# Band attention and a GELU MLP on one core: sums of w_out's quarters by pieces, k of units 12 to 23 split in GpSimd's transfers, and a new order from unit 4 on

## The chip, the cores and the metric

The kernel runs on one NeuronCore of a Trainium2 chip. The metric is device time in microseconds (us) of one launch. Of the kernel before, the median of three runs is 560.4 us (560.36, 560.40 and 560.89).

Engines work side by side, each on its own queue, strictly in the order in which its instructions were issued: TensorE (PE; its weight loads are a column of their own, PEld), VectorE (DVE), ScalarE (ACT), GpSimd (POOL), and SyncE (SP), which issues most DMAs here.

## The reference

Attention over batch 4, 8 heads, 768 positions, head size 64; its output is cut into 3072 rows of 512 and goes through a two-layer MLP.

```python
k_sum = k.reshape(B, H, nb, block, D).max(axis=3)      # block = 32, nb = 24
v_sum = v.reshape(B, H, nb, block, D).mean(axis=3)
scores_l = where(|i - j| < 16, scale * q @ k.T, -1e9)  # the band
scores_s = scale * q @ k_sum.T + log(block)            # the summaries
a = softmax(concat([scores_l, scores_s]));  attn = a @ concat([v, v_sum])
x = attn.transpose(0, 2, 1, 3).reshape(3072, 512)
h = x @ w_in                                           # 512 -> 2048
g = 0.5 * h * (1 + erf(h / sqrt(2)))
out = g @ w_out                                        # 2048 -> 512
```

## The kernel before, in words

**Attention** is cut into 24 units of 256 queries by 4 heads. From unit 6 on (units 0 to 5 are f32) every f32 operand is split into two f16 parts, "hi" (the rounded value) and "lo" (what is left), and every product is three f16 products: hi by hi, hi by lo, lo by hi. A unit's steps are: load q, k, v; make their hi and lo parts; `scores` (TensorE, L861) into pss; `add_mask` (VectorE, L881); `maximum` (GpSimd); `shift` (VectorE, L895); `exponent` (ScalarE, L898); `s_p_hi` (ScalarE, L906) and `p_lo` (VectorE, L910); `sums` (TensorE, L959) and `values` (TensorE, L943); then `norm_take`, `norm_cross`, `norm_rec`, `norm_spread`, `norm_mult` (L966 to L993) divide by the sums, and `x_hi`, `x_lo` write the MLP's input xos. q of units 12 to 23 is split without VectorE: `q_cast` (GpSimd DMA that casts to f16, L829), `q_neg` (ScalarE, the negative, L833), `q_acc` (GpSimd DMA that adds the f32 values onto it, L836). k of all units comes by a DMA from SP (`load_k`, L689), its hi part on ScalarE (`s_k_hi`, L758), its lo part on VectorE (`k_lo`, L818). The maxima of k blocks (`prep_k`, L610, and `prep_k_end`) are copied beside k by `k_sums` (L623), once for the three units that share it.

**The MLP** works on 3072 tokens: six batches of 512 (0 to 5), of which the first two are worked on in four chunks of 256. Weights come as raw f32 and are cut into bits: `wi_bits` and `wo_bits` (L477, L482, L486), `wi_hi`, `wi_lo` (L512, L515), `wo_hi`, `wo_lo` (L572, L575). For w_out there are eight pieces, each 128x1024 f32. Chunks 0 to 3's first layer is `phase1` (L1020 to L1022, three products a row) into psh, then `gelu`, `g_hi`, `g_lo`; `phase2` (L1139 to L1141) into pso is the second layer of chunks 0 to 5 (batch 2 makes chunks 4 and 5), read by `store`. The first layer of batches 2 to 5 is done by Strassen's seven products: `xsum`, `xs_hi`, `xs_lo` (L1052 to L1063) make sums of x; `sp` (L1091) multiplies into psx, psy and psz; `snap` (L1102, ScalarE) empties a psy; `comb` or `h_comb` (L1109, L1194, VectorE) adds up; `h_gelu`, `h_sum`, `h_hi`, `h_lo` (L1199 to L1218) make the left operands of the second layer. Its second layer for batches 3, 4 and 5 is Strassen too: `so` (L1375) multiplies into pso_y, pss_x, psv_z and others; `o_snap` (L1397, ScalarE) empties a "y" accumulator into g_os; `o_sum` (L1404, VectorE) adds another accumulator to it; `o_out` (L1411) and `o_put` end it. In "so b n q j", b is the batch, n the product, q the quarter of the inner dimension, j the half of the columns; in "sp b q n" and "snap b q n", n is the product.

**Sums of w_out's quarters** are operands of that second layer. Before, they are made from w_out's hi and lo parts in SBUF: `t_sum q i` (32 VectorE additions of 128x512, L1295 and L1300), `t_hi`, `t_lo` (16 each, 128x512, L1328 and L1331), `ts` (16 DMAs into t_dram); `tl`, `tr` and `t1_load` load them back.

**What sets the order.** All steps stand in one hand-written list, `ORDER` (L79 to L272), some 2000 steps such as "so 3 7 3 1". They are issued in this order, and each engine runs its share in it. A step that has to wait holds everything behind it on the same engine. Buffers come from `SLOTS` (L273), digits that say which of a pool's buffers each new tile takes.

Of the kernel before, what the change touches and what calls it, by code (L numbers as in the profile page):

```python
# [103 lines left out]
prep_k 2 1, wo_bits 2 0, g_lo 1 3, wo_bits 2 1, norm_rec 4, phase2 0 0, wo_bits 2 2, g_lo 0 2, norm_spread 4,
load_mask, gelu 1 2, load_q 7, fetch_w_out 3 5, gelu 1 0, g_hi 1 0, wo_bits 3 0, gelu 0 7, prep_k_end 1 0, wo_bits 3
1, g_lo 1 1, wo_bits 3 2, phase1 0 6, phase1 1 7, k_sums 1 0, k_lo 6, load_vs 5, g_hi 1 2, fetch_w_out 4 4, shift 5,
s_q_hi 7, phase2 0 1, gelu 0 6, norm_mult 4, wo_hi 3, wo_hi 2, exponent 5, wo_lo 3, phase1 1 6, wo_bits 4 0,
fetch_w_out 5 5, wo_lo 2, wo_bits 4 1, scores 6, f_sums 5, evac 6, wo_bits 5 0, wo_bits 4 2, x_hi 4, wo_bits 5 1,
f_values 5, wo_hi 4, norm_take 5, norm_cross 5, wo_bits 5 2, wo_lo 4, f_mask 7, wo_hi 5, load_k 7, wo_lo 5, norm_rec
5, norm_spread 5, phase2 0 3, fetch_v 1 2, phase2 0 2, phase2 0 4, g_lo 1 0, x_lo 4, gelu 1 7, maximum 6, phase2 0 5,  # L110
load_v 7, norm_mult 5, q_lo 7, x_hi 5, g_hi 0 7, x_lo 5, s_k_hi 7, g_hi 0 6, g_lo 0 7, fetch_w_out 6 4, g_lo 1 2,
fetch_w_out 7 5, gelu 1 6, g_hi 1 7, fetch_k 1 2, shift 6, prep_v 1 2, wo_bits 6 0, phase1 2 6, g_lo 1 7, phase1 2 4,
gelu 2 6, exponent 6, gelu 2 4, phase1 2 0, g_hi 1 6, prep_k 1 2, wo_bits 7 0, load_v 6, k_lo 7, g_lo 0 6, prep_k_end
1 1, gelu 2 0, g_lo 1 6, load_k 9, s_p_hi 6, wo_bits 7 1, phase1 2 1, gelu 2 1, wo_bits 6 1, wo_bits 7 2, p_lo 6,
fetch_v 1 1, wo_bits 6 2, load_q 9, k_sums 1 1, phase1 2 7, fetch_v 1 0, wo_hi 7, wo_hi 6, s_q_hi 9, wo_lo 7, wo_lo 6,
scores 7, s_k_hi 9, sums 6, fetch_v 1 3, prep_v 1 1, q_lo 9, prep_v 1 0, fetch_k 2 0, fetch_v 2 1, prep_v 1 3, phase1
2 3, k_lo 9, fetch_k 2 3, load_vs 6, g_hi 2 4, phase2 0 6, store 0 0, phase2 0 7, g_hi 2 1, g_lo 2 1, g_lo 2 4,
norm_take 6, evac 7, load_q 8, prep_k 2 0, prep_v 2 1, phase2 1 0, g_hi 2 6, phase2 1 2, phase2 1 4, gelu 2 3, gelu 2
7, prep_k 2 3, norm_cross 6, load_vs 7, v_hi 6, maximum 7, load_k 8, wt_add 1 0, g_hi 2 7, v_hi 7, s_k_hi 8, wt_add 1
1, v_lo 6, fetch_v 2 2, shift 7, s_q_hi 8, v_lo 7, exponent 7, norm_rec 6, scores 9, values 6, load_v 9, prep_k_end 2  # L120
0, phase2 1 6, k_lo 8, q_lo 8, norm_spread 6, load_k 11, g_hi 2 3, prep_v 2 2, add_mask 9, s_p_hi 7, p_lo 7, load_q
11, maximum 9, norm_mult 6, wt_add 1 2, x_hi 6, phase1 2 5, g_lo 2 6, phase1 2 2, put 0 0, wt_hi 1, store 1 0, s_q_hi
11, scores 8, x_lo 6, gelu 2 5, add_mask 8, load_v 8, sums 7, norm_take 7, load_vs 9, norm_cross 7, put 1 0, wt_lo 1,
g_lo 2 7, fetch_k 2 2, shift 9, s_k_hi 11, norm_rec 7, q_lo 11, maximum 8, gelu 2 2, values 7, g_hi 2 2, v_hi 9,
phase2 1 1, norm_spread 7, phase2 1 3, store 0 1, g_hi 2 5, norm_mult 7, k_lo 11, x_hi 7, g_hi 2 0, g_lo 2 2, x_lo 7,
phase2 1 5, shift 8, exponent 8, v_lo 9, phase1 3 2, prep_k 2 2, g_lo 2 5, s_p_hi 8, phase2 1 7, load_q 10, p_lo 8,
s_q_hi 10, wt_add 0 0, g_lo 2 0, load_vs 8, v_hi 8, exponent 9, load_k 10, fetch_v 2 0, v_lo 8, load_v 11, phase1 3 4,
s_k_hi 10, sums 8, g_lo 2 3, scores 11, add_mask 11, load_v 10, wt_add 0 1, values 8, put 0 1, q_lo 10, wt_add 0 2,
phase1 3 5, gelu 3 2, load_vs 10, k_lo 10, norm_take 8, s_p_hi 9, p_lo 9, phase1 3 6, maximum 11, wt_hi 0, norm_cross
8, sums 9, scores 10, norm_rec 8, norm_spread 8, q_cast 12, load_k 12, gelu 3 6, store 1 1, norm_mult 8, gelu 3 5,  # L130
prep_v 2 0, load_vs 11, x_hi 8, add_mask 10, v_hi 10, values 9, norm_take 9, wt_lo 0, ws 0, norm_cross 9, g_hi 3 6,
put 1 1, shift 11, g_hi 3 2, gelu 3 4, x_lo 8, fetch_v 2 3, exponent 11, phase1 3 1, norm_rec 9, norm_spread 9, s_p_hi
11, norm_mult 9, maximum 10, q_neg 12, v_hi 11, k_sums 2 0, phase1 3 7, v_lo 10, phase2 2 1, g_lo 3 2, phase2 2 3,
shift 10, phase1 3 0, wt_add 2 0, v_lo 11, load_v 12, exponent 10, g_hi 3 5, p_lo 11, g_lo 3 5, sums 11, values 11,
phase2 2 5, s_k_hi 12, x_hi 9, prep_v 2 3, prep_k_end 2 1, gelu 3 0, k_lo 12, wt_add 2 1, wt_add 3 0, q_cast 13,
wt_add 2 2, k_sums 2 1, x_lo 9, norm_take 11, s_p_hi 10, p_lo 10, wt_add 3 1, q_acc 12, wt_hi 2, g_hi 3 0, scores 12,
gelu 3 1, phase2 2 7, g_lo 3 6, g_lo 3 0, add_mask 12, q_neg 13, norm_cross 11, load_vs 12, v_hi 12, g_hi 3 4,
norm_rec 11, load_k 13, wt_add 3 2, q_acc 13, norm_spread 11, maximum 12, sums 10, norm_mult 11, s_k_hi 13, norm_take
10, store 2 1, phase1 3 3, norm_cross 10, gelu 3 3, k_lo 13, phase2 2 0, v_lo 12, shift 12, sp 2 0 1, exponent 12,
norm_rec 10, g_hi 3 3, values 10, x_hi 11, wt_lo 2, load_v 13, s_p_hi 12, sp 2 0 2, load_k 15, snap 2 0 1, scores 13,  # L140
norm_spread 10, load_v 15, wt_add 6 0, wt_hi 3, x_lo 11, gelu 3 7, q_cast 15, norm_mult 10, put 2 1, fetch_k 3 3, p_lo
12, add_mask 13, phase2 2 2, phase2 2 4, xsum 2 1, xsum 2 3, xs_hi 2 3, g_hi 3 1, s_k_hi 15, xsum 2 2, wt_lo 3, xs_hi
2 2, g_lo 3 4, q_cast 14, sums 12, g_hi 3 7, sp 2 1 1, snap 2 1 1, phase2 2 6, xs_hi 2 1, comb 2 0 0, sp 2 1 2, prep_k
3 3, load_vs 13, v_hi 13, norm_take 12, store 2 0, k_lo 15, norm_cross 12, xs_lo 2 2, xs_lo 2 3, values 12, maximum
13, shift 13, t_sum 0 3, xsum 2 4, g_lo 3 3, wt_add 5 0, exponent 13, ws 1, s_p_hi 13, g_lo 3 1, wt_add 5 1, v_lo 13,
q_neg 15, comb 2 1 0, wt_add 6 1, load_k 14, norm_rec 12, sp 2 0 6, fetch_k 3 1, put 2 0, wt_add 5 2, prep_k 3 1,
s_k_hi 14, xs_hi 2 4, wt_add 6 2, k_lo 14, q_acc 15, snap 2 0 2, q_neg 14, load_v 14, phase2 3 0, phase2 3 2, wt_hi 6,
wt_add 7 0, xs_lo 2 1, load_k 17, wt_lo 6, sp 2 1 6, wt_add 4 0, sp 2 0 7, wt_hi 5, sp 2 0 5, p_lo 13, wt_add 7 1,
snap 2 1 2, snap 2 0 3, s_gelu 2 0 0, fetch_k 3 0, norm_spread 12, wt_add 4 1, phase2 3 4, s_gelu 2 1 0, norm_mult 12,
wt_add 4 2, q_acc 14, wt_hi 4, sums 13, xs_lo 2 4, comb 2 0 3, scores 15, sp 2 0 4, g_lo 3 7, s_k_hi 17, wt_lo 5,  # L150
wt_lo 4, s_gelu 2 0 2, sg_hi 2 1 0, phase2 3 6, norm_take 13, store 3 0, load_vs 15, sg_lo 2 1 0, k_lo 17, sp 2 1 5,
phase2 3 1, wt_add 7 2, norm_cross 13, load_vs 14, wt_hi 7, prep_k 3 0, sg_hi 2 0 2, norm_rec 13, add_mask 15, sp 2 0
3, wt_lo 7, scores 14, values 13, sg_lo 2 0 2, comb 2 0 1, s_gelu 2 0 3, fetch_v 3 0, v_hi 15, add_mask 14, sp 2 1 7,
# [1376 lines left out]
```

## Time and profile before

| what | value |
| --- | --- |
| median of three runs | 560.4 us |
| profiled execution | 560.75 us |
| its span | 558.9 us |
| TensorE (PE) busy | 549.5 us, 98% |
| VectorE (DVE) busy | 484.0 us, 87% |
| ScalarE (ACT) busy | 389.7 us, 70% |
| GpSimd (POOL) busy | 110.8 us, 20% |
| DMA packets' share of 16 engines, SP's queue | 43.3% |
| DMA packets' share, GpSimd's queue | 5.0% |

The span is the time from the first to the last recorded work on the core; 1.85 us of the profiled execution's own time lie around it. An engine's busy time is the union of its instructions' times, so matmuls that overlap are not counted twice. The granted clock of TensorE is 1.00 in all slices, its upper level of 2.4 GHz. Most rows are read as "start, duration, engine, line, operation, output <- input, shape, count"; a bracket at the end holds the idle time in front and what ended it. Durations of neighbours on one engine overlap at their ends by about 0.1 us.

### The profile page before, as it was taken

The page shows a single profiled execution, that of the slowest core. Times are in us where ns is not written, and L with a number is a line of the kernel's source. Part 1 is how long each engine was busy: PE and PEld are TensorE (multiplying, and loading weights), DVE is VectorE, ACT ScalarE, POOL GpSimd, SP SyncE. Part 2 cuts the span into 40 slices and gives each one's busy share as a digit, 9 for nine tenths or more (in the row PEclk, how much of TensorE's full clock was granted, in tenths as well). Part 3 has the DMA queues.
Part 4 walks back from the last instruction along what each step waited for, and adds up shares of the span by engine and source line. Part 5 has one row for each costly group of instructions (what it writes and reads, how often), then busy time and mean ns, then how long its engine had stood idle before and what let it go on. Part 6 is the DMA issues. An engine that isn't in the chain of part 4 may idle for free.

```text
span 558.9 us, 14486 instructions
## 1 busy us (share of the span) xinstructions
PE 549.5 (98%) x6155; PEld 414.8 (74%) x6155; DVE 484.0 (87%) x680; ACT 389.7 (70%) x677; POOL 110.8 (20%) x66
## 2 busy tenths in 40 slices
...
GB/s 328 396 285 380 166 173 178 280 116 221 157 146 171 153 143 187 133 65 182 127 167 149 154 115 89 90 145 200 256 207 150 60 94 1 1 1 29 48 1 86
DMA packets 42640, 84.26 MB, mean 151 GB/s; under 512 B 4176, under 2 KB 16720, under 8 KB 42064
## 3 DMA queue, kind: packets, MB, share of 16 engines
q1 hardware_dynamic: 38832, 79.85, 43.3%
...
q14 instruction: 16, 0.13, 0.1%
...
## 4 chain that ended last, share of the span: by engine, by line
PE 81%; DVE 13%; DMA 3%; issue 1%; ACT 1%; SPq 0%; DVEq 0%
PE psy L1091 15%; PE pso_y L1375 8%; PE psz L1091 8%; PE pso L1139 7%; PE pso L1140 7%; PE pso L1141 6%; PE psx L1091 4%; PE psd_y L1375 4%; PE pss_x L1375 4%; PE psv L943 3%; PE psh L1020 3%; PE psh L1021 2%; PE psh L1022 2%; PE pss L861 2%; PE psv_z L1375 2%; DMA w_out_h<-in_vt_dram 2%
## 5 line engine op out<-in xcount | busy, mean ns | idle before, releaser
L890 POOL PARTITION_ALL_REDUCE m<-s x23 | 82.0, 3567 | 187.4 <-DVE w_out_l L575 40.1
L1091 PEld LDWEIGHTS <-wt 128*128 128x128 f16 x768 | 74.3, 98 | 10.2 <-issue 0.2
L1139 PE MATMUL pso<-w_out_h,gg 128*128 128x512 f16 x192 | 72.9, 379 | 0.0
L1141 PE MATMUL pso<-w_out_h,gg 128*128 128x512 f16 x192 | 72.8, 379 | 0.0
L1140 PE MATMUL pso<-w_out_l,gg 128*128 128x512 f16 x192 | 72.8, 379 | 0.0
L1021 PE MATMUL psh<-xos,ww 128*128 128x256 f16 x256 | 69.8, 273 | 0.8 <-DVE xos L1000 0.8
L1091 PE MATMUL psy<-xos,wt 128*128 128x256 f16 x576 | 70.5, 273 | 0.0
L1020 PE MATMUL psh<-xos,ww 128*128 128x256 f16 x256 | 69.8, 273 | 0.1
L1022 PE MATMUL psh<-xos,ww 128*128 128x256 f16 x256 | 69.8, 273 | 0.0
L1091 PEld LDWEIGHTS <-ww 128*128 128x128 f16 x576 | 55.8, 98 | 8.9 <-issue 0.4
L1375 PEld LDWEIGHTS <-gg 128*128 128x128 f16 x576 | 55.8, 98 | 7.7 <-issue 1.1
L1102 ACT ACTIVATE ww<-psy 128x512 f32<-128x512 f32 x48 | 28.3, 591 | 27.4 <-PE psy L1091 27.3
L1141 PEld LDWEIGHTS <-gg 128*128 128x128 f16 x192 | 18.7, 98 | 22.8 <-issue 0.4
L1139 PEld LDWEIGHTS <-gg 128*128 128x128 f16 x192 | 18.7, 98 | 19.8 <-issue 0.4
L1140 PEld LDWEIGHTS <-gg 128*128 128x128 f16 x192 | 18.8, 98 | 19.1
L1375 PEld LDWEIGHTS <-wt 128*128 128x128 f16 x288 | 28.1, 98 | 3.4 <-issue 0.2
L1218 DVE SCALAR_TENSOR_TENSOR gg<-h,gg 128x512 f16<-128x512 f32 x32 | 21.4, 686 | 10.1 <-ACT gg L1215 9.9
L1020 PEld LDWEIGHTS <-ww 128*128 128x128 f16 x256 | 25.0, 98 | 4.3 <-issue 0.4
L1022 PEld LDWEIGHTS <-ww 128*128 128x128 f16 x256 | 25.0, 98 | 4.1 <-issue 1.2
L1021 PEld LDWEIGHTS <-ww 128*128 128x128 f16 x256 | 25.0, 98 | 3.7
L1029 ACT ACTIVATE g<-psh 128x512 f32<-128x512 f32 x32 | 19.0, 593 | 11.4 <-DVE gg L1038 8.6
L895 DVE TENSOR_TENSOR s<-s,m 128x1024 f32<-128x1024 f32 x21 | 25.5, 1216 | 0.1
...
## 6 DMA issues: line engine op xcount, KB each, us to landing
...
```

The source lines that it names most:

```text
L890: nc.gpsimd.partition_all_reduce(out_ap=self.m32, in_ap=self.s32, channels=P, reduce_op=bass_isa.ReduceOp.max)
L895: nc.vector.tensor_tensor(out=self.s32, in0=self.s32, in1=self.m32, op=ALU.subtract)
L1020: nc.tensor.matmul(ph[:, e, :], wh, xh, start=(k == 0), stop=False)
L1021: nc.tensor.matmul(ph[:, e, :], wh, xl, start=False, stop=False)
L1022: nc.tensor.matmul(ph[:, e, :], wl, xh, start=False, stop=(k == NCC - 1))
L1091: nc.tensor.matmul(ps[:, e, :], ws, xx, start=(first and e == 0 and k == 0 and m == 0), stop=(k == 1 and m == 2), skip_group_check=True,)
L1102: nc.scalar.activation(snaps[b, q, n], split8(acc[b, q, "y"]), AF.Copy)
L1139: nc.tensor.matmul(p, gh, w_out_h[:, f, :], start=(f == 0), stop=False)
L1140: nc.tensor.matmul(p, gh, w_out_l[:, f, :], start=False, stop=False)
L1141: nc.tensor.matmul(p, gl, w_out_h[:, f, :], start=False, stop=(f == NFC - 1))
L1218: nc.vector.scalar_tensor_tensor(out=a_part(b, q, m, 1), in0=h_src(b, q, m), scalar=SC_G, in1=a_part(b, q, m, 0), op0=ALU.mult, op1=ALU.su ...
L1375: nc.tensor.matmul(ps, g, ww_, start=(first and e == 0 and k == 0), stop=(e == 1 and k == 2), skip_group_check=True,)
```

## The change

1. `wo_put f` stores each f32 piece of w_out to a DRAM tile `wo_dram` when it has been cut (8 DMAs of 512 KB). `tw_load f` loads it back later, and `t_sum f i` (four VectorE operations of 128x256 per piece), `t_hi f` (ScalarE, 128x1024) and `t_lo f` (VectorE, 128x1024) work on a piece. `ts f` stores hi and lo of all four sums at once into `t_dram`, now one tile with the positions `TPOS`. The old `t_sum q i` and its followers go.
2. k of units 12 to 23: `k_cast` (GpSimd DMA that casts k to f16 straight into k_hi, from an input `k96` of 128x960 with room for the summaries), `k_neg` (ScalarE), `k_acc` (GpSimd DMA that adds), and `k_sum` (ScalarE, the summaries' hi part, per unit). `load_k`, `s_k_hi` and `k_lo` of these units go.
3. `M16_ROOM` and `ks_f` use the room of w_out's lo part; `ks16` has four buffers in place of two; the clearing of k_hi and k_lo takes all 32 last columns; GpSimd's DMA scratch is 1024 in place of 512.
4. `ORDER` is written anew from after "wo_bits 0 2" (unit 4, about 58 to 77 us by engine), and `SLOTS` with it.

```diff
+TPOS = {1: 1, 2: 0, 3: 3, 4: 2}
 ORDER = '''
-fetch_k 2 1, wi_bits 7 1, wo_hi 0, wo_bits 1 0, gelu 1 4, g_lo 0 1, wi_bits 7 2, phase1 1 3, gelu 1 1, fetch_w_out 2
...
+wi_bits 7 1, load_q 6, k_lo 6, phase1 1 3, gelu 1 1, g_hi 1 1, fetch_k 1 1, g_lo 0 3, phase1 1 5, wo_put 0, g_lo 0 1,
...
+    def wo_put(f):
+        queue[0].dma_start(out=wo_dram[:, f], in_=sts[f])
...
     def k_sums(b, r):
         for i, a in enumerate((k_hi[r], k_lo[r])):
+            if b >= 2 and i == 0:
+                continue
...
+        def k_cast(self):
+            nc.gpsimd.dma_start(out=k_hi[self.u % UPC].rearrange("p t j -> p (t j)"), in_=k96[self.u])
+
+        def k_sum(self):
+            nc.scalar.activation(
+                self.kh[:, :, 0:CT, SLOT_SUM : SLOT_SUM + NBLK],
+                ks16[self.b, self.h0 // UH][:, 0].unsqueeze(2).broadcast_to([P, NR, CT, NBLK]), AF.Copy,
+            )
+
+        def k_neg(self):
+            nc.scalar.activation(self.kl[:, :, :, 0:TQ], self.kh[:, :, :, 0:TQ], AF.Copy, scale=-1.0)
+
+        def k_acc(self):
+            nc.gpsimd.dma_start(out=k_lo[self.u % UPC].rearrange("p t j -> p (t j)"), in_=k96[self.u], accum_op=ALU.add)
...
-    def t_sum(q, i):
-        def tmp(k):
...
+    tws, tst = {}, {}
+
+    def tw_load(f):
+        tws[f] = wk.tile([P, WP], F32, tag="f4k", bufs=N_F4K, name=f"tw_{f}")
+        queue[0].dma_start(out=tws[f], in_=wo_dram[:, f])
+
+    def t_sum(f, i):
+        w = tws[f].rearrange("p (k n) -> p k n", k=4)
+        o, x, y, op = (
+            (w[:, 3], w[:, 3], w[:, 1], ALU.subtract), (w[:, 1], w[:, 1], w[:, 0], ALU.subtract),
+            (w[:, 0], w[:, 3], w[:, 0], ALU.add), (w[:, 2], w[:, 2], w[:, 0], ALU.subtract),
+        )[i]
+        nc.vector.tensor_tensor(out=o, in0=x, in1=y, op=op)
...
+    def ts(f):
+        q, e = f // 2, f % 2
+        queue[0].dma_start(out=t_dram[:, q, :, :, e * CH : (e + 1) * CH], in_=tst[f])
```

Line numbers of the changed kernel are higher by 3 to 30 than those before: `so` L1379 for L1375, `o_snap` L1401 for L1397, `o_sum` L1408 for L1404, `snap` L1127 for L1102, `h_gelu` L1224 for L1199, `exponent` L923 for L898, `wo_lo` L583 for L575.

**ScalarE, around o_snap 3 2 and o_snap 3 3** (g_os_2 and g_os_3, near 390 to 400 us in the trace of before; s_21 and ph are exponent and s_p_hi of unit 21, xos are hi parts of x sums, ks_3_1 the summaries of k_sum 23). Before:

```order
L1397 ACTIVATE g_os_2_6114<-pso_y_5492 128x256
L1059 ACTIVATE xos<-x32s 128x512
L833 ACTIVATE ql_6191<-qh_6034 128x512
L1059 ACTIVATE xos<-x32s 128x512
L1397 ACTIVATE g_os_2_6114<-pso_y_5492 128x256
L1059 ACTIVATE xos<-x32s 128x512
L898 ACT_TABLE_LOAD
L898 ACTIVATE s_21_5864<-s_21_5864 128x1024
L1397 ACTIVATE g_os_3_6287<-pso_y_5492 128x256 x2
```

After:

```order
L1401 ACTIVATE g_os_2_6100<-pso_y_5520 128x256
L1022 ACTIVATE xos<-x32s 128x512
L1084 ACTIVATE xos<-x32s 128x512 x2
L923 ACT_TABLE_LOAD
L923 ACTIVATE s_21_5886<-s_21_5886 128x1024
L931 ACTIVATE ph_6232<-s_21_5886 128x1024
L852 ACTIVATE k_all<-ks_3_1_4590 128x2x4x24
L1401 ACTIVATE g_os_3_6250<-pso_y_5520 128x256 x2
```

Between the last g_os_2 and the first g_os_3 there were three rows; now there are seven instructions.

**ScalarE, around snap 4 0 3 and the gelu table load** (near 413 us; ww<-psy_0 are snaps of batch 4's quarter 0, h_4_0_0 is h_gelu 4 0 0, gg its h_hi). Before:

```order
L915 ACTIVATE vh_6483<-v_23_6106 128x1024
L1102 ACTIVATE ww<-psy_0_6317 128x512
L898 ACTIVATE s_23_6430<-s_23_6430 128x1024
L906 ACTIVATE ph_6573<-s_23_6430 128x1024
L1102 ACTIVATE ww<-psy_0_6317 128x512
L1199 ACT_TABLE_LOAD
L1199 ACTIVATE h_4_0_0_6436<-h_4_0_0_6436 128x512
```

After:

```order
L923 ACTIVATE s_22_6185<-s_22_6185 128x1024
L1127 ACTIVATE ww<-psy_0_5940 128x512
L1224 ACT_TABLE_LOAD
L1224 ACTIVATE h_4_0_0_6533<-h_4_0_0_6533 128x512
L1240 ACTIVATE gg<-h_4_0_0_6533 128x2x256
L1127 ACTIVATE ww<-psy_0_5940 128x512
```

The last snap of psy_0 ahead of sp 4 0 4 stood ahead of the table load; now the load, h_gelu 4 0 0 and its h_hi stand ahead of it.

**VectorE, the end of the program** (the four sums of batch 5's second layer). Before:

```order
L1218 SCALAR_TENSOR_TENSOR gg<-h_5_3_3_7926,gg 128x2x256
L1404 SCALAR_TENSOR_TENSOR g_os_1_8065<-pss_x_7975,g_os_1_8065 128x512
L1404 SCALAR_TENSOR_TENSOR g_os_3_8230<-psv_z_8193,g_os_3_8230 128x512
L1404 SCALAR_TENSOR_TENSOR g_os_2_8158<-psv_z_8193,g_os_2_8158 128x512
L1404 SCALAR_TENSOR_TENSOR g_os_2_8158<-pss_x_7975,g_os_2_8158 128x512
```

After:

```order
L1243 SCALAR_TENSOR_TENSOR wt<-h_5_2_0_7766,wt 128x512
L1408 SCALAR_TENSOR_TENSOR g_os_3_8178<-psv_z_7992,g_os_3_8178 128x512
L1408 SCALAR_TENSOR_TENSOR g_os_1_8018<-pss_x_7939,g_os_1_8018 128x512
L1408 SCALAR_TENSOR_TENSOR g_os_2_8136<-psv_z_7992,g_os_2_8136 128x512
L1408 SCALAR_TENSOR_TENSOR g_os_2_8136<-pss_x_7939,g_os_2_8136 128x512
```

The sum that empties pss_x (o_sum 5 0, into g_os_1) was first of the four and is now second, behind the one of psv_z (o_sum 5 3, into g_os_3).

**VectorE, between the first two low pieces of w_out** (from 66 us on; w_out_l is wo_lo, wst the cut of a piece, ww wi_lo, dent and x32s the norm steps of unit 4). Before:

```order
L575 SCALAR_TENSOR_TENSOR w_out_l<-wst_849,w_out_h 128x1024
L1038 SCALAR_TENSOR_TENSOR gg<-g_0_3_805,gg 128x512
L486 SCALAR_TENSOR_TENSOR wst_962<-x32s,wst_962 128x1024
L1038 SCALAR_TENSOR_TENSOR gg<-g_1_4_964,gg 128x512
L515 SCALAR_TENSOR_TENSOR ww<-wt,ww 128x8x128 x2
L824 TENSOR_TENSOR ql_1073<-q_6_1058,qh_1070 128x512
L575 SCALAR_TENSOR_TENSOR w_out_l<-wst_962,w_out_h 128x1024
```

After:

```order
L583 SCALAR_TENSOR_TENSOR w_out_l<-wst_845,w_out_h 128x1024
L482 TENSOR_SCALAR wst_1033<-x32s 128x1024
L1007 RECIPROCAL rc_1020<-rc_1020 128x16
L487 SCALAR_TENSOR_TENSOR wst_1033<-x32s,wst_1033 128x1024
L491 SCALAR_TENSOR_TENSOR wt<-gg,wt 128x1024
L491 SCALAR_TENSOR_TENSOR wst_1033<-x32s,wst_1033 128x1024
L618 TENSOR_REDUCE ks_1_663<-kp_1_986 128x24
L1011 STREAM_TRANSPOSE dent_1018<-rc_1020 128x512
L618 TENSOR_REDUCE ks_2_1071<-kp_1_1030 128x24
L1018 TENSOR_TENSOR x32s<-psv_908,dent_1018 128x512
L583 SCALAR_TENSOR_TENSOR w_out_l<-wst_1033,w_out_h 128x1024
```

Other steps of the cut, of the maxima and of the norm stand between the two pieces now, in place of two wi_lo and a q_lo.

## Rows read from the trace of the kernel before

**Rows 1.** Busy time by stretch of the span, with count, granted clock, DMA share, GB/s.

```profile
60.00:107.00 47.00, 45.75 (x479) 32.95 (x477) 46.77 (x57) 31.64 (x51) 9.49 (x3) 1.00 0.60 210
107.00:390.00 283.00, 282.54 (x3389) 197.92 (x3388) 273.90 (x394) 226.27 (x386) 69.14 (x38) 1.00 0.53 145
```

**Rows 2.** Waits of TensorE from 60 to 558 us: total, times, longest.

```profile
PE psn L804 <- ACT s L898: 1.0, 1, 1.0
PE pso_y L1375 <- ACT g_os L1397: 0.5, 1, 0.5
PE psh L1021 <- DVE xos L1000: 0.5, 1, 0.5
```

**Rows 3.** The chain that ended last: start, duration, engine, tile, line, count.

```profile
200.88 1.31 PE psy L1091 x12
...
203.06 1.42 PE psx L1091 x12
```

**Rows 4.** A VectorE group by line and shape: busy us, mean ns, idle before.

```profile
L818 DVE TENSOR_TENSOR k_all<-k,k_all 128x640 f16<-128x640 f32 x20 | 17.0, 852 | 0.0
```

**Rows 5.** VectorE's timeline from 74 to 81 us: start, duration, instruction.

```profile
74.45 2.35 DVE L515 SCALAR_TENSOR_TENSOR ww<-wt,ww 128x1024 f16<-128x1024 f32 x2
76.72 0.68 DVE L824 TENSOR_TENSOR ql<-q,qh 128x512 f16<-128x512 f32 x1
77.32 1.22 DVE L575 SCALAR_TENSOR_TENSOR w_out_l<-wst,w_out_h 128x1024 f16<-128x1024 f32 x1
...
79.06 1.80 DVE L610 TENSOR_REDUCE ks<-kp 128x24 f32<-128x768 f32 x2
```

**Rows 6.** TensorE's timeline at 79.6 us, the first phase2 block.

```profile
79.61 0.38 PE L1139 MATMUL pso<-w_out_h,gg 128*128 128x512 f16 x1
```

**Rows 7.** ScalarE's timeline from 391 to 400 us.

```profile
391.92 0.38 ACT L1397 ACTIVATE g_os<-pso_y 128x256 f32<-128x256 f32 x1 [1.48 <-PE pso_y L1375]
392.20 0.62 ACT L1059 ACTIVATE xos<-x32s 128x512 f16<-128x512 f32 x1
...
399.78 0.38 ACT L1397 ACTIVATE g_os<-pso_y 128x256 f32<-128x256 f32 x1 [1.58 <-PE pso_y L1375]
```

**Rows 8.** ScalarE groups by line and shape, columns as in rows 4.

```profile
L906 ACT ACTIVATE ph<-s 128x1024 f16<-128x1024 f32 x18 | 18.9, 1052 | 2.6 <-issue 1.8 <-PE psv L943 0.5
...
L623 ACT ACTIVATE k_all<-ks 128x192 f16<-128x192 f16 x16 | 4.9, 352 | 0.7 <-DVE ks L618 0.6
```

**Rows 9.** ScalarE's timeline from 413 to 416 us.

```profile
413.23 0.60 ACT L1102 ACTIVATE ww<-psy 128x512 f32<-128x512 f32 x1 [0.29 <-PE psy L1091]
413.85 1.28 ACT L1199 ACT_TABLE_LOAD   x1
415.14 1.15 ACT L1199 ACTIVATE h<-h 128x512 f32<-128x512 f32 x2
```

**Rows 10.** TensorE's timeline from 395 to 401 us.

```profile
395.00 2.78 PE L1375 MATMUL pso_y<-wt 128*128 128x256 f16 x24
397.62 1.47 PE L1091 MATMUL psy<-xos,ww 128*128 128x256 f16 x12
398.93 0.82 PE L1375 MATMUL pso_y<-wt,gg 128*128 128x256 f16 x6
400.22 1.47 PE L1375 MATMUL pso_y<-wt,gg 128*128 128x256 f16 x12 [0.47 <-ACT g_os L1397]
```

**Rows 11.** VectorE's timeline at 411 us.

```profile
410.94 0.69 DVE L1194 TENSOR_TENSOR h<-psx,ww 128x512 f32<-128x512 f32 x1 [0.54 <-PE psx L1091]
```

**Rows 12.** TensorE's timeline at 416 us: sums between two blocks.

```profile
415.75 0.29 PE L959 MATMUL psn<-ph,ones 128*32 128x256 f16 x4
...
416.08 0.83 PE L1375 MATMUL pso_y<-wt,gg 128*128 128x256 f16 x6
```

**Rows 13.** VectorE's timeline at 550 us.

```profile
549.77 1.29 DVE L1404 SCALAR_TENSOR_TENSOR g_os<-psv_z,g_os 128x512 f32<-128x512 f32 x2 [4.62 <-PE psv_z L1375]
```

**Rows 14.** GpSimd's q_acc transfers (L836), from issue to landing.

```profile
DMA to landing us min/median/max: 3.6/4.3/7.0
```

More of the change, by code (lines that the diff above doesn't have):

```diff
@@ L104 @@
[L104 to L153, printed above, removed]
@@ new lines @@
+fetch_k 2 3, wt_add 1 0, prep_k 2 0, store 0 0, load_vs 6, load_vs 7, load_q 8, norm_rec 6, wt_add 1 1, prep_v 2 1,
+s_k_hi 9, k_lo 9, phase2 1 0, evac 7, norm_spread 6, v_hi 6, maximum 7, prep_k 2 3, v_lo 6, phase1 2 6, put 0 0,
+s_q_hi 8, phase2 1 2, q_lo 8, shift 7, scores 9, wt_add 1 2, fetch_v 2 2, values 6, add_mask 9, v_hi 7, exponent 7,
+phase2 1 4, v_lo 7, s_p_hi 7, p_lo 7, g_hi 2 7, g_lo 2 1, wt_hi 1, wt_lo 1, phase2 1 6, prep_v 2 2, store 1 0, load_k
+11, sums 7, gelu 2 6, scores 8, load_q 11, s_q_hi 11, load_v 8, fetch_k 2 2, put 1 0, norm_mult 6, load_v 9, norm_take
@@ new lines @@
+7, s_k_hi 11, maximum 9, gelu 2 2, q_lo 11, k_lo 11, phase2 1 1, add_mask 8, shift 9, load_q 10, norm_cross 7,
+norm_rec 7, norm_spread 7, values 7, x_hi 6, prep_k 2 2, x_lo 6, phase1 2 5, store 0 1, load_k 10, maximum 8, scores
+11, g_hi 2 6, norm_mult 7, exponent 9, load_vs 8, x_hi 7, wt_add 0 0, v_hi 8, x_lo 7, phase2 1 3, phase2 1 5, load_vs
+9, shift 8, put 0 1, s_q_hi 10, g_hi 2 2, g_lo 2 6, phase1 3 0, s_k_hi 10, wt_add 0 1, exponent 8, g_lo 2 2, s_p_hi 8,
+q_cast 12, gelu 3 0, phase1 3 6, v_lo 8, p_lo 8, sums 8, values 8, q_lo 10, g_lo 2 7, fetch_v 2 0, add_mask 11, v_hi
```

376 lines of the change are left out of this document (197 added, 179 removed).

## Prediction

> **What bounds the kernel now.** I read the stretches first. From 107 us on TensorE is busy almost without a gap: 282.54 of the 283.00 us from 107 to 390 [rows 1]. From 60 to 107 it is VectorE that has no room: 46.77 of 47.00 us, with TensorE at 45.75. Granted clock is 1.00 in both. Then I read what TensorE waits for after 60 us: three waits of 1.0, 0.5 and 0.5 us [rows 2]. The first and the last of them lie in the VectorE stretch (softmax and MLP input of the first batch); the middle one, pso_y behind g_os, lies at 400 us. So all that TensorE could win back after 60 us is 2.0 us, because the matmuls themselves are the same before and after: the order lists hold the same set of them. What decides is therefore not how much VectorE and ScalarE work goes away, but whether the new order makes TensorE wait somewhere.
>
> A third view, the chain that ended last, gives the price of mixing shapes on TensorE: a block of 12 matmuls of 128x256 takes 1.31 us, but 1.42 right behind a block of another shape [rows 3]. A change of shape costs about 0.1 us.
>
> **Part 1: less work on VectorE and ScalarE.** Twelve k_lo go (0.85 us each [rows 4], 10.2 us), and the sums of w_out's quarters are made as 32 sums half as wide and 8 wide lo parts, in place of 32 sums and 16 lo parts. ScalarE trades 12 k_hi for 12 k_neg of the same size. All of it lies between 107 and 400 us, where TensorE did not wait for either engine [rows 1, 2]. Taken off, it takes nothing off the end: **0 us**. What covers it is TensorE's own 282.54 us, and that cover does not go away.
>
> **Part 2: the stretch from 66 to 107 us.** Here VectorE is the bound, and the first phase2 block needs the second low piece of w_out (wo_lo 1). The order shows what stands ahead of it from 66.03 us on. Gone are two lo parts of w_in (2.35 us) and a lo part of q (0.60) [rows 5]. New are k_lo 6 (0.77 without the overlap with its neighbour), two maxima of k blocks (1.80), a transpose and a product of 128x512, put at the 0.68 of q's lo part, which is as wide, [rows 4, 5] and a small reciprocal. That is 3.93 in and 2.95 out, so wo_lo 1 ends 1.0 us later than now, at 79.5 in place of 78.5 [rows 5]. TensorE now comes to its first phase2 block at 79.61 [rows 6]; in the new order one block of phase1 (24 matmuls of 0.109, 2.6 us) stands behind it, so it comes at 77.0 and to the second piece half a block later, at 78.3. So by 80 us it has waited about 1.2 us. By the end of the stretch (107 us) the same blocks are done in both. In the old order the two waits of this stretch cost 1.5 [rows 2]; the new one has 1.2 and, since wo_lo 3 and 4 stand close to their readers again, something like 0.2 or 0.4 more. Term: **0 us**, between -1.0 (nothing after the first wait, and part of that hidden behind another late reader) and +1.0 (each of the later two pieces as late as the first).
>
> **Part 3: changes of shape.** Going through TensorE's rows from the first attention unit in split form on, I count the places where scores, sums, values and the wide blocks follow one another: 92 before, 99 after. Fewer of the short blocks stand together (sums then scores 5 to 1, scores then values 5 to 1). Seven times 0.1 [rows 3]: **+0.7 us**, and none of it is hidden, since TensorE is the chain.
>
> **Part 4: three places where a TensorE block now waits for a queue.**
>
> (C) At 395 us, batch 3's last block of the 3 7 product (pso_y) may start when o_snap 3 3 has emptied the accumulator. On ScalarE that copy now stands behind three x copies, the exp table load, exponent 21, s_p_hi 21 and k_sum 23; before, behind one x copy, the load and the exponent. From the row of the snap ahead of them [rows 7] on: 0.38 + 3 x 0.62 + 1.28 [rows 9] + 1.05 + 1.05 + 0.35 [rows 8] + 0.38 is 6.35; neighbours overlap by 0.1 at six of the joins (391.92 + 0.38 against 392.20 [rows 7]), so 5.75. A snap starts 0.20 after TensorE has left the block that it reads (398.93 + 6 x 0.109 = 399.58, against 399.78), and TensorE goes on 0.06 after the copy (399.78 + 0.38 = 400.16, against 400.22) [rows 7, 10]. Together 6.0. TensorE has 42 matmuls meanwhile, 0.109 each (24 take 2.62 [rows 10]): 4.6. It waits **1.4 us**. The wait of 0.5 at 400 us stays: o_snap 3 3 1 again stands right behind so 3 4 0 0.
>
> (D) At 414 us sp 4 0 4 waits for snap 4 0 3. Before, this snap stood ahead of the gelu table load; now it stands behind the load, h_gelu 4 0 0 and h_hi. The chain: 0.20 + h_comb 0.69 [rows 11] + 0.06 + load 1.28 + 0.53 + 0.53 + snap 0.60 [rows 9] + 0.06 = 3.95. TensorE's cover is 12 matmuls (1.31), the sums (0.33 [rows 12]) and 12 more behind a change of shape (1.42): 3.06. It waits **0.9 us**.
>
> (E) At 548 us so 5 3 2 1 (pss_x) needs o_sum 5 0, which VectorE now does behind o_sum 5 3. Before, o_sum 5 0 was first of the four and long done. Two such sums take 1.29 [rows 13], with 0.20 ahead and 0.06 behind 1.55; TensorE has 7 matmuls, 0.76. It waits **0.8 us**. Nothing behind it gives that back: these are the last 10 us.
>
> A rule of the Trainium skill speaks about C and D. In the row, the load ends at 415.13 and the gelu starts at 415.14 [rows 9]: nothing lies behind the load. The Trainium skill ("ScalarE: Activation LUTs", What ACT_TABLE_LOAD costs) gives 1.28 us for the load and a drain of 1.38 beside it. The trace agrees with the first and shows no drain; by the page C and D would each be 1.4 larger and the time 567.0.
>
> **Part 5: GpSimd's k transfers.** 24 more transfers go through its queue. A q transfer lands 4.3 us after its issue, 3.6 to 7.0 [rows 14]. A k transfer writes 240 KB where q's writes 128, so I bound its landing between 3.6 (all fixed) and 13 (7.0 x 1.9). The shortest way from k_acc to its scores is unit 12's: two phase1 blocks (5.2 us), a phase2 block (2.6), sums and values between them, about 9 us. With 4.3 scaled whole, 8.1, it is just covered; the next leads are longer than 9.6. Term **0 us**, up to +4 at unit 12 (13 - 9).
>
> **The sum.** 0 + 0.7 + 1.4 + 0.9 + 0.8 = +3.8 us. The profiled execution took 560.75 (span 558.9), the median of the runs is 560.4, 0.35 less; so 560.75 + 3.8 - 0.35 = **564.2 us**.
>
> **Rivals.**
> - *Late k transfers on top: 566 to 568.* The order gives unit 12 9 us, and landing may be up to 13. Decides from a landing of 9 us on. Against it: the median row of q. For it: the Trainium skill ("SBUF — State Buffer", SBUF: two separate sides) says that some VectorE copies lock GpSimd out of writing its transfers' descriptors, 620 ns alone against 3100 overlapped. What rows show is a landing of q's that goes up to 7.0 while VectorE is busy nearly all the time.
> - *A drain behind each table load: 567.0*, as the page has it; the row at 415.14 speaks against it.
> - *No change: about 561.* Each of C, D and E is counted from one row's end, and TensorE's cover may be longer than the matmuls I put there. If two of the three are hidden, by 0.9 us more cover at each, and the first stretch comes out 1.0 better, the sum is -0.5 to +1.
> - *Faster: about 559.0.* The place is 66 to 107 us: if wo_lo 1 comes at 78.3 or before, and the later pieces with it, TensorE waits nowhere there, -1.5, and with no shape cost felt and C to E hidden the time is 558.9 to 559.2. It decides when the VectorE queue ahead of wo_lo 1 is 1.2 us shorter than the rows make it and C, D and E together stay under 0.4. I see a reason for the first (a row's overlap) and none for the second.
>
> **How the numbers follow.** This forecast, all or most of the three waits: 0.58. Late transfers on top: 0.13. Drain: 0.02. No change: 0.15. Faster: 0.12. The measurement can tell about 0.2% (1.1 us) from nothing. Faster 0.12, same 0.15, slower 0.73. The range runs from 560.5, inside the case of no change, to 568.0, where the late transfers end.
>
> **What would show it.** Right: rows for TensorE's waits of about 1.4 on g_os near 395, 0.9 on ww near 414 (both pso_y and psy), 0.8 on g_os near 548, and none over 0.5 between 107 and 390. In the first stretch wo_lo 1 ending about 79.5. Wrong: a wait on k_all or pss in front of scores 12 or 14 (transfers), rows between load and gelu (drain), or a stretch from 60 to 107 with less than 0.5 us of waits.

## The result: 0.7% slower, and the profile after

The changed kernel takes 564.14 us (median of four runs, 563.96 to 565.23), the kernel before 560.38 (four runs). The ratio is 1.0067, its 95% interval 1.0053 to 1.0081: 3.8 us slower, where 3.8 was forecast (564.2). The profiled execution took 563.96 us with a span of 562.2, 3.2 more than the span before.

The stretches of the changed kernel, with the columns of [rows 1]:

```profile
60.00:107.00 47.00, 46.13 (x474) 32.63 (x475) 46.97 (x59) 32.93 (x55) 7.91 (x3) 1.00 0.68 232
107.00:390.00 283.00, 283.00 (x3391) 197.67 (x3389) 265.89 (x375) 226.70 (x383) 82.98 (x64) 1.00 0.74 183
390.00:420.00 30.00, 27.22 (x334) 22.96 (x333) 21.64 (x30) 18.84 (x31) 6.44 (x2) 1.00 0.46 148
```

From 107 to 390 us VectorE is 8.0 us lighter than in [rows 1] and GpSimd 13.8 heavier. TensorE stood still for 0.46 us there before (the wait at 108.5 us) and for nothing after, so the lighter VectorE had next to nothing to buy. From 390 to 420 TensorE stands still for 2.8 us.

What TensorE waited for, from 60 to 562 us (the view of [rows 2]):

```profile
PE pso_y L1379 <- ACT g_os L1401: 1.9, 2, 1.4
PE psy L1116 <- ACT ww L1127: 0.9, 1, 0.9
PE pss_x L1379 <- DVE g_os L1408: 0.8, 1, 0.8
PE psh L1045 <- ACT g L1054: 0.5, 1, 0.5
```

And where these are on TensorE's timeline (a bracket: idle time in front and what ended it):

```profile
397.52 0.81 PE L1379 MATMUL pso_y<-wt 128*128 128x256 f16 x6 [1.43 <-ACT g_os L1401]
402.34 0.82 PE L1379 MATMUL pso_y<-wt,gg 128*128 128x256 f16 x6 [0.47 <-ACT g_os L1401]
416.37 1.47 PE L1116 MATMUL psy<-xos,wt 128*128 128x256 f16 x12 [0.87 <-ACT ww L1127]
...
550.73 0.27 PE L1379 MATMUL pss_x<-w_out_h,wt 128*128 128x256 f16 x1 [0.79 <-DVE g_os L1408]
```

C is there with 1.43 (1.4 forecast), D with 0.87 (0.9), E with 0.79 (0.8), and the 0.47 of [rows 10] is still there. These idle times are counted from the end of a matmul that lasts 0.27 us, though the next may start after 0.109; counted from start to start they are 0.16 longer. That gives 1.59, 1.04 and 0.96.

**The bill.** Counted that way through both traces, start to start:

| part | forecast | measured |
| --- | --- | --- |
| head, before the orders part (differs from run to run) | 0 | -0.87 |
| 60 to 109 us, with the wait of 0.6 that lay there before | 0 | -0.06 |
| changes of shape from 107 us on, 90 before, 96 after | +0.7 | +0.57 |
| C | +1.4 | +1.59 |
| D | +0.9 | +1.04 |
| E | +0.8 | +0.96 |
| sum | +3.8 | +3.23 (span: +3.2) |

The head is that of one execution: the matmul that starts at 64.87 us in the trace of before starts at 64.19 to 64.25 in e3, e6 and e9, whose order is the same up to there. Without the head the parts add up to 4.1, and the medians differ by 3.76; the 0.3 between them is of the size by which single runs differ.

### The profile page after: what moved, and what is told of

Read it like the earlier page. It is cut to its first block, busy times and chain, and to the rows that moved or that the text cites. A ratio compares the mean times of both kernels' runs of the same rounds, so it can differ in the third digit from the quotient of the medians.

```text
span 562.2 us, 14499 instructions
## 1 busy us (share of the span) xinstructions
PE 551.5 (98%) x6155; PEld 414.3 (74%) x6155; DVE 472.2 (84%) x660; ACT 392.0 (70%) x679; POOL 123.2 (22%) x90
## 3 DMA queue, kind: packets, MB, share of 16 engines
q0 software_dynamic: 6912, 9.05, 12.9%
## 4 chain that ended last, share of the span: by engine, by line
PE 82%; DVE 10%; DMA 3%; issue 2%; ACT 2%; SPq 0%; DVEq 0%; ACTq 0%
PE psy L1116 15%; PE psz L1116 7%; PE pso L1164 7%; PE pso L1165 7%; PE pso L1166 7%; PE pso_y L1379 7%; PE pss_x L1379 4%; PE psx L1116 4%; PE psd_y L1379 4%; PE psv L968 3%; PE psh L1045 3%; PE psh L1046 3%; PE psh L1047 3%; PE pss L886 3%; PE psv_z L1379 2%
## 5 line engine op out<-in xcount | busy, mean ns | idle before, releaser
L915 POOL PARTITION_ALL_REDUCE m<-s x23 | 77.1, 3354 | 142.8 <-ACT s L902 41.8
L1379 PEld LDWEIGHTS <-gg 128*128 128x128 f16 x576 | 56.0, 98 | 7.4 <-issue 0.9
L1127 ACT ACTIVATE ww<-psy 128x512 f32<-128x512 f32 x48 | 28.2, 589 | 24.3 <-PE psy L1116 18.6
L1379 PEld LDWEIGHTS <-wt 128*128 128x128 f16 x288 | 28.1, 98 | 5.9 <-issue 2.6
L943 DVE SCALAR_TENSOR_TENSOR vl<-v,vh 128x1024 f16<-128x1024 f32 x18 | 25.8, 1437 | 1.1 <-ACT vh L940 1.1
```

The costliest lines, as they stand in the source:

```text
L915: nc.gpsimd.partition_all_reduce(out_ap=self.m32, in_ap=self.s32, channels=P, reduce_op=bass_isa.ReduceOp.max)
L943: nc.vector.scalar_tensor_tensor(out=self.vl, in0=self.v32.rearrange("p n d -> p (n d)"), scalar=SC_X, in1=self.vh, op0=ALU.mult, op1=ALU. ...
L1127: nc.scalar.activation(snaps[b, q, n], split8(acc[b, q, "y"]), AF.Copy)
L1379: nc.tensor.matmul(ps, g, ww_, start=(first and e == 0 and k == 0), stop=(e == 1 and k == 2), skip_group_check=True,)
```

## The experiments

Ratios are to the kernel before, run on the same chip beside each kernel. The changed kernel's own is 1.0067.

### e1: only the queues cleared

```diff
-exponent 21, s_p_hi 21, xsum 4 4, k_sum 23, ... so 3 7 3 0, o_snap 3 3 0, tl 3 2 4, so 3 7 3 1
+xsum 4 4, k_sum 23, ... so 3 7 3 0, o_snap 3 3 0, exponent 21, s_p_hi 21, tl 3 2 4, so 3 7 3 1
-o_sum 5 3, o_put 5 3 0, o_put 4 3 1, so 5 3 0 0, o_sum 5 0
+o_put 4 3 1, so 5 3 0 0, o_sum 5 0, o_sum 5 3, o_put 5 3 0
```

> The changed kernel, with two waits' queues cleared and nothing else moved: exponent 21 and s_p_hi 21 stand behind o_snap 3 3 0 (so only three x copies, the table load and k_sum 23 are ahead of it), and o_sum 5 0 stands ahead of o_sum 5 3. Theory of the prediction (queues): the wait near 396 us (1.43 in the changed kernel) goes to 0 and the one near 549 us (0.81) to at most 0.1, since o_sum 5 0 no longer has a sum ahead of it; time 564.1 - 2.1 = 562.0. Rival (the block that waits writes the tile that the copy still reads, so the wait has a floor: 0.20 until the copy starts, 0.38 or 0.69 for the copy, 0.06 back): the wait near 396 falls to 0.5 to 0.65 and the one near 549 stays at 0.8; time 563.3.

Measured: 564.81 us, ratio 1.0079 (1.0058 to 1.0100). TensorE's timeline from 390 to 420 us, then its last wait and VectorE's row there:

```profile
396.81 0.82 PE L1379 MATMUL pso_y<-wt 128*128 128x256 f16 x6 [0.47 <-ACT g_os L1401]
401.63 0.81 PE L1379 MATMUL pso_y<-wt,gg 128*128 128x256 f16 x6 [0.47 <-ACT g_os L1401]
405.78 0.22 PE L968 MATMUL psv<-ph,vl 128*64 128x64 f16 x2 [0.76 <-DVE vl L943]
416.72 1.47 PE L1116 MATMUL psy<-xos,wt 128*128 128x256 f16 x12 [0.87 <-ACT ww L1127]
```

```profile
550.02 0.27 PE L1379 MATMUL pss_x<-w_out_h,wt 128*128 128x256 f16 x1
551.07 0.27 PE L1379 MATMUL pss_x<-w_out_h,wt 128*128 128x256 f16 x1 [0.78 <-DVE g_os L1408]
```

```profile
550.33 0.69 DVE L1408 SCALAR_TENSOR_TENSOR g_os<-pss_x,g_os 128x512 f32<-128x512 f32 x1 [12.18 <-PE pss_x L1379]
550.93 1.28 DVE L1408 SCALAR_TENSOR_TENSOR g_os<-psv_z,g_os 128x512 f32<-128x512 f32 x2
```

The rival was right at both places. VectorE had been idle for 12.18 us and takes o_sum 5 0 first, and TensorE still waits 0.78. The sum can't start before so 5 3 0 0 has ended (0.20 behind its last matmul): it stands behind it in the order, and both touch the same accumulator tile, whose halves are products 2 and 3 (the sum reads product 2's, the blocks write product 3's). So E was never the queue; o_sum 5 3 ahead of it cost 0.01. At C the wait falls to 0.47, the same as the old one at 400 us, and no further: so 3 7 3 1 follows the copy of the tile that it goes on writing (in its other half). Of C's 1.43 the queue was 0.96 and this floor 0.47. The time did not fall to the rival's 563.3, because a new wait of 0.76 came, on v's lo part of unit 21; from start to start it is 0.93, about what C lost. Exponent 21 now comes later, and behind it p_lo 21, add_mask 23 and GpSimd's maximum 23 (402.76 us for 400.56 in the changed kernel). v_lo 21, which took 1.22 there, ran beside this maximum and took 2.61:

```profile
403.12 2.61 DVE L943 SCALAR_TENSOR_TENSOR vl<-v,vh 128x1024 f16<-128x1024 f32 x1
```

```profile
402.76 3.22 POOL L915 PARTITION_ALL_REDUCE m<-s  x1 [7.73 <-DVE s L906]
```

### e2: all three waits taken away by order

```diff
-exponent 21, s_p_hi 21, xsum 4 4, k_sum 23, ... so 3 7 3 0, o_snap 3 3 0, tl 3 2 4, so 3 7 3 1
+k_sum 23, exponent 21, s_p_hi 21, xsum 4 4, ... so 3 7 3 0, so 3 7 3 1, o_snap 3 3 0, tl 3 2 4
-h_comb 4 0 0, sums 23, h_gelu 4 0 0, ... h_hi 4 0 11, snap 4 0 3
+h_comb 4 0 0, snap 4 0 3, sums 23, h_gelu 4 0 0, ... h_hi 4 0 11
-so 5 2 3 1, ... so 5 3 0 0, o_sum 5 0
+so 5 2 3 1, o_sum 5 0, ... so 5 3 0 0
```

> The changed kernel with its three waits taken away by order alone: so 3 7 3 1 ahead of o_snap 3 3 0 (and k_sum 23 ahead of exponent 21), snap 4 0 3 ahead of the gelu table load, o_sum 5 0 ahead of so 5 3 0 0 by several blocks. If the waits C, D and E are what the change costs at its end, the three rows (1.43, 0.87, 0.81) are gone and the time is 564.1 - 3.1 = 561.0, between 560.7 and 561.4; the 0.47 near 400 us stays. If something else makes up for them (later waits that they hid), less than 1.5 us comes back: 562.6 or more.

Measured: 560.80 us, ratio 1.0016 (1.0001 to 1.0031), so 0.5% less than the changed kernel. TensorE's waits from 60 us on:

```profile
PE psh L1045 <- ACT g L1054: 0.5, 1, 0.5
PE pso_y L1379 <- ACT g_os L1401: 0.5, 1, 0.5
```

The three are gone and nothing took their place. Four moved steps out of 1936 give back 0.51% (1.0067 less 1.0016), 2.9 us of the 3.8, give or take some 1.1 by the two intervals; the two traces' spans differ by 3.5.

### e3: the kernel before without twelve k_lo

```diff
-k_lo 12 ... k_lo 23
```

> The kernel before, with the 12 lo parts of k of units 12 to 23 left out (the scores of these units are then not the reference's): 10.2 us less on VectorE between 150 and 410 us, nothing else moved. The prediction says that relief of VectorE there is worth 0: 560.4, within 0.3, and the same three waits of TensorE. The rival, that VectorE (97% busy in this stretch) holds TensorE up in ways that the waits do not show, gives 558 to 559.

Measured: 560.10 us, ratio 0.9998 (0.9986 to 1.0009). VectorE is 6.7 us lighter from 107 to 390 us (267.23 for 273.90), 7.6 to 410 us, less than the 10.2 expected, and the three waits of [rows 2] are what they were. That is VectorE's saving of part 2 of the change, without its cost, and it is worth nothing here.

### e4: one GpSimd transfer later

```diff
-k_acc 12, norm_take 11, ... k_sums 2 0, maximum 10, scores 12
+norm_take 11, ... k_sums 2 0, maximum 10, k_acc 12, scores 12
```

> The changed kernel with one GpSimd transfer, k_acc 12, issued behind the maximum of unit 10, some 3.5 us later (at 185.4 in place of 181.9 us of the trace); scores 12 begin at 190.95. By the rival of late transfers as it was bounded before (8.1 us from issue to landing), TensorE waits 2.6 us before scores 12. By the landing that the changed kernel's trace shows for k_acc (median 5.8, least 4.8), it waits 0 to 0.3 us, and 2.0 at the longest landing seen (7.6).

Measured, one run: 571.33 us. TensorE at scores 12 and behind:

```profile
195.91 0.29 PE L886 MATMUL pss<-qh,k_all 64*128 64x64 f16 x4 [4.65 <-DMA k_all<-in_k_dram]
```

GpSimd, and the granted clock (the third-last number) by stretches of 4 us:

```profile
188.88 1.81 POOL L861 DMA_DIRECT2D k_all<-in_k_dram  x2 [3.32 <-ACT rc L999]
```

```profile
186.00:190.00 4.00, 4.00 (x27) 2.40 (x25) 3.96 (x8) 3.23 (x10) 1.12 (x3) 1.00 0.12 16
190.00:194.00 4.00, 1.27 (x54) 0.95 (x52) 0.92 (x1) 3.94 (x4) 1.56 (x2) 1.00 0.94 242
194.00:198.00 4.00, 2.09 (x48) 1.81 (x49) 0.69 (x1) 1.65 (x4) 0.42 (x1) 0.55 1.03 127
198.00:202.00 4.00, 4.00 (x24) 2.86 (x22) 3.96 (x5) 0.00 (x0) 1.35 (x2) 0.60 0.49 68
202.00:206.00 4.00, 4.00 (x31) 2.19 (x30) 3.40 (x7) 1.44 (x3) 2.45 (x2) 1.00 0.21 24
```

My place for it was wrong: the transfer was now behind k_sums 2 0 too, a ScalarE copy into the same buffer (at 188.16 us), so it was issued at 188.88 and not at 185.4 (the bracket names the ScalarE row right behind that copy). It landed after 7.0 us, inside the range. The wait was 4.65 us, and the time rose by 7.2: behind the wait the granted clock is 0.55 and 0.60 for 8 us, and the phase1 block there (24 matmuls) took 4.74 us in place of 2.80. So a miss of GpSimd's transfers would have been dearer than I had priced it, and the new order leaves this one 9.05 us (issued at 181.90, needed at 190.95), 1.5 more than the longest landing of a k_acc in its trace (7.6; 8.1 in e4's).

### e5 and e6: narrow blocks joined, and the wait near 400

```diff
 e5, on top of e2
-values 7, x_hi 6, ... maximum 8, scores 11
+x_hi 6, ... maximum 8, values 7, scores 11
-scores 13, sp 2 1 1, values 10
+sp 2 1 1, scores 13, values 10
-sums 13, sp 2 0 7, add_mask 15, scores 14
+sp 2 0 7, add_mask 15, sums 13, scores 14
... and so sums 17, values 17, scores 19; sums 18, values 18; sums 20, scores 22
-so 3 5 3 0, ... add_mask 23, o_snap 3 3 1, so 3 4 0 1
+o_snap 3 3 1, so 3 5 3 0, ... add_mask 23, so 3 4 0 1
 e6, on the kernel before
-o_snap 3 3 0, so 3 4 0 0, ... norm_rec 20, o_snap 3 3 1
+o_snap 3 3 0, o_snap 3 3 1, so 3 4 0 0, ... norm_rec 20
... and joined: values 10, scores 13; sums 18, scores 20; sums 19, values 19
```

> The kernel of e2 (the changed kernel without waits C, D and E), with o_snap 3 3 1 ahead of so 3 5 3 0 as well (the 0.47 near 400 us) and seven narrow blocks of TensorE (scores, sums or values) moved by one to four blocks so that they stand beside another narrow one: 104 changes of shape become 97. Theory: 0.47 and 7 x 0.1 go, 560.8 - 1.2 = 559.6, the same as or a little under the kernel before. If a change of shape costs nothing of its own, 560.3.

> The kernel before with o_snap 3 3 1 ahead of so 3 4 0 0 (its 0.47 near 400 us) and three narrow blocks moved beside others (98 changes of shape become 95). Theory: 0.47 + 0.3 go, 560.2 - 0.8 = 559.4. If the wait near 400 comes back elsewhere, 560.

Measured: e5 560.45 us, ratio 0.9997 (0.9986 to 1.0009); e6 559.80 us, ratio 0.9991 (0.9981 to 1.0001). From e2 to e5 that is 0.19%, 1.1 us where 1.2 was forecast, but the two intervals overlap, and the rival lies only 0.7 from the forecast, so the times alone decide nothing. The traces do: from the same matmul near 105 us to the last one e5 takes 449.04 us, e2 450.19. In e5's trace 89 changes of shape from 107 us on took 10.6 us beyond the matmuls' own pace, in e2 and the changed kernel 96 took 11.25: 0.1 each (the expectations count over the whole order). The 0.47 went too, and a new wait of 0.25 on g_os came at 380.77 us. In e6 the 0.47 also went, but the next block then came too early for a load, as its rival had it:

```profile
407.40 1.49 PE L1091 MATMUL psy<-xos,wt 128*128 128x256 f16 x12 [0.73 <-DMA wt<-wt_dram]
```

### e7: two maxima cut short in the changed kernel

```diff
-    in_=kt[:, :, WINDOW:].rearrange("p r (n j) -> p r n j", j=BLOCK), axis=AX.X, op=ALU.max
+    in_=kt[:, :, WINDOW:].rearrange("p r (n j) -> p r n j", j=BLOCK)[:, :, :, : 2 if (b, g) in ((1, 1), (2, 1)) else BLOCK],
+    axis=AX.X, op=ALU.max
```

> The changed kernel, with two of VectorE's maxima of k blocks (prep_k 1 1 and prep_k 2 1, 0.87 us each, both ahead of wo_lo 1) taken over 2 of the 32 positions, so the summaries of these k are not the reference's: 1.5 us less on VectorE ahead of wo_lo 1. Theory (from 66 to 107 us VectorE sets the pace): the small waits on w_out's low pieces (0.27 near 78.5, and those near 94 and 102) go, and the phase1 wait on gelu (0.54 near 71) stays: 0.3 to 0.9 less, 563.2 to 563.8. Rival (ScalarE or the transfers set it): no change, 564.1.

Measured: 563.24 us, ratio 1.0054 (1.0040 to 1.0068), 0.7 us under the changed kernel by the ratios, whose intervals overlap. The traces are clearer: the matmul at 104.89 us in the changed kernel comes at 104.11, and from there to the last one both take the same (453.58 and 453.59). The wait on gelu stays (0.53) and the phase2 blocks, which held the small waits, run through. In the new order VectorE does set the pace ahead of w_out's low pieces.

### e8 and e9: towards a faster kernel

```diff
 e8 and e9, on top of e6
-wr 3 0 1, ... norm_cross 21, wr 3 0 0, sp 4 0 6
+wr 3 0 0, wr 3 0 1, ... norm_cross 21, sp 4 0 6
 e8 only (SLOTS is fitted to it)
-wo_bits 0 2, fetch_k 2 1, ... prep_k 1 1, prep_k 2 1, wo_bits 2 0
+wo_bits 0 2, ... prep_k 1 1, wo_bits 2 0, ... prep_k 2 0, fetch_k 2 1, ... prep_k 2 3, prep_k 2 1
```

> The kernel of e6 with two more moves: the load wr 3 0 0 earlier in SyncE's queue (e6 waited 0.73 for it near 407 us), and prep_k 2 1, a maximum of 0.87 us on VectorE, with its load taken out of the stretch from 66 to 107 us and put near 135 us, where TensorE does not wait for VectorE. Theory (that stretch is paced by VectorE, and the late wait was SyncE's order): the waits of 1.0 and 0.5 in the stretch fall by 0.9 together and the 0.73 goes, 559.8 - 1.6 = 558.2 to 558.8, faster than both kernels. Rival (the wait comes back where the maximum now stands, or ScalarE paces the stretch): 559.5 or more.

> The kernel of e6 with one more move: the load wr 3 0 0 ahead of wr 3 0 1 in SyncE's queue, so that sp 4 0 6 no longer waits 0.73 for it near 407 us; nothing moved from 66 to 107 us. Theory: e6's remaining loss was that load, 0.73 goes and no wait of TensorE is left between 107 and 558 us: ratio to the kernel before 0.9991 - 0.0013 = 0.9978, 559.0 to 559.3. Rival (the wait reappears at the next block that needs a slot): 559.8.

Measured: e8 563.41 us, ratio 1.0059 (1.0045 to 1.0072); e9 558.95 us, ratio 0.9979 (0.9967 to 0.9991). e8 failed twice over. The waits of 1.0 and 0.5 in the first stretch stayed, so in the old order 0.9 us less on VectorE there moves nothing (what paces them was not followed further). And at the maximum's new place TensorE waited 1.99 us for v's lo part. VectorE's rows ahead of that lo part show how:

```profile
135.78 0.95 DVE L610 TENSOR_REDUCE ks<-kp 128x24 f32<-128x768 f32 x1 [1.80 <-DMA kp<-in_kp_dram]
136.65 0.68 DVE L540 TENSOR_TENSOR t<-wt 128x512 f32<-128x512 f32 x1
137.37 2.00 DVE L546 TENSOR_TENSOR t<-wt,t 128x256 f32<-128x256 f32 x1
```

VectorE stood 1.80 us for the maximum's own load, which had been moved with it, and the sum of L546, which takes 0.42 at this step in e6's trace, took 2.00 beside a GpSimd maximum; the moved maximum itself is 0.95. So e8 shows that this place was bad, not that every later place would be. The clock fell behind the wait as in e4:

```profile
140.00:142.00 2.00, 1.45 (x46) 1.06 (x47) 2.00 (x3) 1.10 (x2) 0.41 (x1) 0.84 0.37 39
142.00:144.00 2.00, 2.00 (x6) 0.70 (x5) 1.97 (x6) 2.00 (x3) 0.00 (x0) 0.50 0.55 223
144.00:146.00 2.00, 2.00 (x11) 0.95 (x10) 2.00 (x3) 0.23 (x1) 0.00 (x0) 0.81 0.45 126
```

e9 is the kernel before with one copy, one load and three narrow blocks moved. TensorE waits only twice from 60 us on, both ahead of 109 us, and it beats both kernels.

## Why the prediction was right, and where it was not

**What bounds the kernel, and parts 1 and 5: right.** TensorE is the chain; VectorE's relief is worth 0 (e3); the transfers are in time. One weight load of TensorE waited 0.2 us for a k_cast, and no matmul waited for any of them. k_acc's landing, from issue (the view of [rows 14]):

```profile
DMA to landing us min/median/max: 4.8/5.8/7.6
```

It writes 1.9 times as much as q_acc and lands after 1.35 times the median of [rows 14], so the end of 13 us that I had from scaling the whole of 7.0 was too far. What I did not foresee is that with 24 more transfers the q transfers land later too: q_acc after 3.6/6.2/9.2 us, q_cast after up to 11.5 (6.8 before), for which ScalarE once waited 2.2. Why is open; the DMA share is up as well (0.74 for 0.53). The Trainium skill ("SBUF — State Buffer", SBUF: two separate sides) has 3.1 us for a GpSimd transfer beside a VectorE copy, 620 ns alone. Nothing like it shows at k_acc's issue: 0.85 to 0.94 us, in a stretch where VectorE is 94% busy (265.89 of 283), though with sums and lo parts more than with copies.

**Part 2: right in the sum, on a detour.** VectorE ended wo_lo 1 at 78.55 us:

```profile
77.34 1.21 DVE L583 SCALAR_TENSOR_TENSOR w_out_l<-wst,w_out_h 128x1024 f16<-128x1024 f32 x1
```

This trace runs 0.87 us ahead of the one before, so that is 79.42 against 79.5 forecast. I had TensorE wait 1.2 us for it. It waited 0.27, since it had already waited 0.54 for gelu 1 4, a ScalarE step behind norm_cross 4, which I had not put in. The last of the old waits, psh on xos, lies at 108.5 us and not before 107, as I had it. Counted to 109 us the stretch is -0.06.

**Part 3: right.** Six changes more from 107 us on, +0.57 in place of +0.7.

**Part 4: the sizes right, two causes wrong in part.** The chain of C is in ScalarE's rows as it was added up:

```profile
391.54 0.39 ACT L1401 ACTIVATE g_os<-pso_y 128x256 f32<-128x256 f32 x1 [2.99 <-PE pso_y L1379]
391.82 0.62 ACT L1022 ACTIVATE xos<-x32s 128x512 f16<-128x512 f32 x1
392.34 1.14 ACT L1084 ACTIVATE xos<-x32s 128x512 f16<-128x512 f32 x2
393.50 1.28 ACT L923 ACT_TABLE_LOAD   x1
394.79 1.06 ACT L923 ACTIVATE s<-s 128x1024 f32<-128x1024 f32 x1
395.89 1.06 ACT L931 ACTIVATE ph<-s 128x1024 f16<-128x1024 f32 x1
396.85 0.35 ACT L852 ACTIVATE k_all<-ks 128x192 f16<-128x192 f16 x1
397.10 0.36 ACT L1401 ACTIVATE g_os<-pso_y 128x256 f32<-128x256 f32 x1
```

391.54 to 397.46, the end of the copy, is 5.92, where 5.75 was forecast. But I took the whole wait for the queue's, and e1 shows that a third of it (0.47 of 1.43) is the order of so 3 7 3 1 behind a copy of its own tile. For E the step "VectorE now does o_sum 5 0 behind o_sum 5 3" was the wrong cause: e1 undid just that and the wait stayed at 0.78. It came from the place of o_sum 5 0 behind so 5 3 0 0; e2 moved it ahead and the wait went. The size came out right because both chains end within 0.1 us of each other: two sums from the end of psv_z, or one sum (0.69, with 0.20 and 0.06) from the end of so 5 3 0 0. The cover was also miscounted: between psv_z and the wait stand six matmuls (0.65), not seven. D is as forecast, chain and cause:

```profile
413.24 1.28 ACT L1224 ACT_TABLE_LOAD   x1 [1.48 <-DVE h L1219]
414.54 0.63 ACT L1224 ACTIVATE h<-h 128x512 f32<-128x512 f32 x1
415.20 0.63 ACT L1240 ACTIVATE gg<-h 128x512 f16<-128x512 f32 x1
415.74 0.58 ACT L1127 ACTIVATE ww<-psy 128x512 f32<-128x512 f32 x1
```

The load at 413.24 ends at 414.52 and the gelu starts at 414.54. The drain of 1.38 us that the Trainium skill gives beside the load ("ScalarE: Activation LUTs", What ACT_TABLE_LOAD costs) is in none of these rows, at C or at D; by the page the time would have been 567.

**The total** is right to 0.1 us, which is luck beyond the terms: the waits were each 0.14 to 0.19 longer than forecast, the shapes a little cheaper.
